# A fused attention, MLP and expert kernel on one core: a form of loads, two rules of its planner and its table of numbers are changed

## The chip, the cores and the metric

The kernel runs on one core of one Trainium2 chip. The core has a matrix engine (PE, with its weight loads PEld), a vector engine (DVE), a scalar engine (ACT), a general engine (POOL) and a queue for transfers (SP), which run side by side and wait for one another by semaphores. The metric is the device time of one execution in microseconds; the median of several runs counts.

## What is computed

Attention on (2, 8, 576, 64), a two-layer MLP with squared ReLU, and a sum over four experts weighted by normalised probabilities. In attention, the first four heads see the last 32 positions (local) and the other four the positions of the same residue modulo 32 (strided).

```python
scores = scale * np.matmul(q, k.transpose(0, 1, 3, 2))
mask_local = (rel >= 0) & (rel < stride)
mask_strided = (rel >= 0) & (pos[None, :] % stride == pos[:, None] % stride)
scores = np.where(masks[None, :, :, :], scores, -1000000000.0)
attn = softmax(scores)
x = np.matmul(attn, v)              # to (1152, 512)
h = np.maximum(x @ w_in, 0.0)       # (512, 2048)
x = h * h @ w_out                   # (2048, 512)
for e in range(4):                  # (512, 1024) and (1024, 512)
    out += p[:, e:e + 1] * (np.maximum(x @ w1[e], 0.0) @ w2[e])
```

## The kernel before

All work is written as tasks with costs and ranks, and a planner in the kernel (class Plan) plays them through when the program is built: each engine takes the ready task of lowest rank for which buffers are free, and the order so found is what each engine executes. The costs in it (SAME, CROSS, FROM_PE and so on are delays between engines in ns) are the author's numbers; they set the order and nothing else. The long table of numbers in the main function holds ranks, buffer counts and switches.

Attention is cut into twelve groups. A strided group covers eight heads times a few residues of one batch (54 or 36 rows of keys and queries in each unit, eight units); a local group covers 192 queries in six units. A group goes through these steps: k, q and v are loaded by SP (lines 459 to 469 for strided groups, 543 to 549 for local ones); PE forms scores (484, 564) into one PSUM bank, with the mask added either by a matmul of constants (478, 558; on_pe_) or by DVE (646, 650); DVE takes the maximum (657); the exponential is either whole (DVE subtracts, 666, ACT does one instruction, 667, DVE sums, 668) or unit by unit (ACT, 661, with the sum on the way); DVE makes the reciprocal (670), POOL or DVE normalises (671); PE transposes (489, 569, 571), ACT or DVE copies the result out (634); PE multiplies with v (501, 581, 586) into one or two banks; ACT and DVE write the result as a high part (682, 684) and a low part (688) into x. Five groups of the first batch are the start-up; five more (one local, three strided, one local) and two last local ones run between the products of the MLP. The start-up groups may use the ba and by banks, the later ones only the two ba banks.

The strided class has two forms. With four=True the v of a group is loaded in two transfers to 64 partitions each, and the value matmuls go to four places (two halves of the contraction by two halves of the output) and two banks. With four=False one transfer with zero padding fills 128 partitions, and the matmuls go to two places and one bank. The start-up uses False, the second batch True.

The MLP works on x in three blocks of 384 tokens (x0, x1, x2). A product is three matmuls (high times high, high times low, low times high; lines 883 to 885). Four products make one H in a bank bh (at first also by); ACT and DVE make the squared ReLU and its two halves h (948 to 961); h enters the second layer's sums in by (y products). Weights come as 512 KB loads into three buffers raw (828) and are split by ACT, DVE and POOL (834, 840, 845, 853, 855, 859). Later stages multiply blocks with fewer products by Strassen-like sums (lines from 1049 on, and the groups of the experts, whose results DVE adds in lines 1376 and 1543). While PE has nothing to do in the start-up the planner puts filler matmuls in (line 1572); their number is fixed when the program is built.

The rule that picks a bank when several rings can serve takes the first ring that has one. set_up (lines 420 to 427) makes the identity and the local masks from the constants cb on DVE; score tasks come after it in the plan.

Of the kernel before, what the change touches and what calls it, by code (L numbers as in the profile page):

```python
# [16 lines left out]
P = 128  # L17
# [56 lines left out]
class Plan:  # L74
# [8 lines left out]

    SAME, CROSS, FROM_PE, TO_PE, DMA = 40, 125, 205, 260, 2200
    FIRST_DMA = 700
# [6 lines left out]
    def __init__(self):  # L92
        self.tasks, self.rings = [], {}
        self.filler = None
        self.tense = set()
        self.shared = 0
# [15 lines left out]
    def run(self):  # L112
# [32 lines left out]
        while done < len(self.tasks):  # L145
# [4 lines left out]
            while events and events[0][0] == now:  # L150
# [4 lines left out]
                elif what == "idle":  # L155
                    idle[x] = True
                elif what == "end":
                    t = x
                    done += 1
                    for env, key in t.free:  # L160
                        ring, tile_ = env["_", key]
                        self.rings[ring].append(tile_)
                    for ring, tiles in t.adds:
                        self.rings[ring] += tiles
                    for y in then.get(t, ()):
                        waits[y] -= 1
                        if y.behind is t or t.ran == "pe" and "pe" in y.engines:
                            lag = 0
                        elif t.ran == "dma":
                            lag = self.DMA  # L170
                        elif t.ran in y.engines:
                            lag = self.SAME
                        else:
                            lag = self.FROM_PE if t.ran == "pe" else self.TO_PE if "pe" in y.engines else self.CROSS
                        ready_at[y] = max(ready_at.get(y, 0), now + lag)
                        if not waits[y]:
                            push(ready_at[y], "ready", (y, None))
            for e in ready:
                while idle[e] and ready[e]:
# [14 lines left out]
                    for env, key, rings in got.take:  # L194
                        r = next(r for r in rings if self.rings[r])
                        tile_ = self.rings[r].pop(0)
# [30 lines left out]
def tile_attention_mlp_experts(ctx: ExitStack, tc: tile.TileContext, a, out):  # L227
# [24 lines left out]
    HOLD = 4828  # L252
    AHEAD = 13299
    END2 = 34373
    END3 = -13679
    CONV = -36244
    R_LOW, R_HI = 5016, 616
    CONV1 = -36491
    CONV2 = 32503
    FETCH = 62728  # L260
    WITH2 = -2960
    PE_SLICE = 1914
    SQ = (0, 20, 0)
    R_MASK = 5624
    ON_PE = (1, 0, 0, 0, 0, 0, 0)
    FILL = 0
    R_MAX = 46387
    R_EXP = -28553
    R_NORM = 34851
    R_T = -64464  # L270
    R_V = -44215
    R_X = -42089
    R_LO = -58785
    R_OUT = -599
    FIRST = (-10664, -21928, 10634, -16154, -76519)
    WHOLE = (1, 1, 0, 0, 1, 1, 1, 1, 1, 1, 1, 0)
    S_T, S_V, S_X = -14699, 658, 1170
    L_T, L_V, L_X = 4928, -8176, -46841
    LKQ = (-9530, -55365, -19117, -7603, -3595)
    LV = (5544, -85907, 1533, 13101, 30113)  # L280
    LW = {('wi', 0, 1): -25050, ('wi', 0, 0): -59935, ('wi', 1, 1): -15643, ('wo', 0, 0): -58033, ('wo', 0, 1): -37919, ('wi', 1, 0): 812}
    EARLY = {('wi', 0, 1): -55765, ('wi', 0, 0): -53381, ('wi', 1, 1): 36780, ('wo', 0, 0): -20896, ('wo', 0, 1): -14224, ('wi', 1, 0): 12953}
    GROUP = 4
    AHEAD_H = 3
    EARLY_H = ((25994, -28049, -26801, 16069), (24535, -56810, 107537, 9733), (-57149, -14711, -28287, 25063), (-38851, -19584, 18159, -9722))
    NRAW = 3
# [6 lines left out]
    NV = 5  # L293
    LEAD = -27857
    L_CB = -31388
    L_ID = 18024
    WI1 = 11088
    NPT = 2
    NW = 10
    NS = 2  # L300
    NTMP = 3
    S_LEAD = -12738
    S_LEAD1 = -12772
    T_LEAD1 = 45954
    U = 2 * GROUPS
# [36 lines left out]
    def mm_r(n):  # L342
        return 229 if n == 512 else int(n / 2.4) + 13

# [64 lines left out]

    t_pe = plan.add({"dma": 500}, load_pe, rank=due(2 * half))  # L410
    t_pe = plan.add({"dve": 700}, weigh, after=[t_pe], rank=due(2 * half) + 8000)

# [191 lines left out]
    def attend(g, rank, rings, lead, early=None, whole=False, on_pe_=1):  # L604
# [33 lines left out]
        masked = on_pe_  # L638
        t = plan.add({"pe": g.cost_s + (mm_r(n) if masked else 0)}, lambda e: g.scores(env, masked), after=[t_cb, t_ci, t_go, *loads[:2], *(transposed[-3:-2] if len(rings) == 1 else [])], rank=rank, take=[(env, "S", rings)], free=[(env, "q"), (env, "k")], tiled=True)
        if not masked:  # L640
# [56 lines left out]
    for k, g in enumerate(startup):  # L697
        attend(g, FIRST[k], ["bank_a", "bank_y"], 0, k, WHOLE[k])
    second = [Local(0, 2)] + [Strided(1, j) for j in range(3)] + [Local(1, 0)]
    for k, g in enumerate(second):  # L700
# [5 lines left out]
    def open_late(e):  # L706
# [7 lines left out]
        for k in range(KD // 2):  # L714
            late["h", k] = late["T", 2][:, :, k]

    t_late = plan.add({"none": 1}, open_late, after=attention_done, rank=0, adds=[("parts", [("parts", 0)])])

# [557 lines left out]
    def open_last(e):  # L1276
        early.close()
        rp = ctx.enter_context(tc.tile_pool(name="last", bufs=1, side="right"))
        for k in range(3):
            late["w2", k] = rp.tile([P, 2, DM], F32R, name=f"o{k}")  # L1280

    t_last = plan.add({"none": 1}, open_last, after=t_sums, rank=0, adds=[("w2", [("w2", k) for k in range(3)]), ("tmp", [("tmp", 0)])])
# [379 lines left out]
```

## Time and profile before

| | us |
|---|---|
| median of 3 runs | 621.35 (620.80 to 621.83) |
| profiled execution | 621.1 |
| its span | 619.3 |
| PE busy | 609.3 (98%) |
| DVE busy | 458.7 (74%) |
| ACT busy | 301.5 (49%) |
| POOL busy | 122.7 (20%) |

The span is the time from the first to the last instruction that the profile shows. Busy time of PE counts overlapping matmuls once. In a time line a row has its start, its length, the engine, the source line, the operation and its tiles, and in square brackets the idle time before it and what ended it; "issue" stands there when the profile shows nothing that it waited for. The TensorE clock granted was at full speed from 4.6 us on.

### The profile page before, as it was taken

The page shows a single profiled execution, that of the slowest core. Times are in us where ns is not written, and L with a number is a line of the kernel's source. Part 1 is how long each engine was busy: PE and PEld are TensorE (multiplying, and loading weights), DVE is VectorE, ACT ScalarE, POOL GpSimd, SP SyncE. Part 2 cuts the span into 40 slices and gives each one's busy share as a digit, 9 for nine tenths or more (in the row PEclk, how much of TensorE's full clock was granted, in tenths as well). Part 3 has the DMA queues.
Part 4 walks back from the last instruction along what each step waited for, and adds up shares of the span by engine and source line. Part 5 has one row for each costly group of instructions (what it writes and reads, how often), then busy time and mean ns, then how long its engine had stood idle before and what let it go on. Part 6 is the DMA issues. An engine that isn't in the chain of part 4 may idle for free.

```text
span 619.3 us, 10613 instructions
## 1 busy us (share of the span) xinstructions
PE 609.3 (98%) x4026; PEld 556.5 (90%) x4026; DVE 458.7 (74%) x893; ACT 301.5 (49%) x688; POOL 122.7 (20%) x148
## 2 busy tenths in 40 slices
PE   8999999999999999999999999999999999999997
PEld 4788999999999999998898989898898989898996
DVE  5988897385787973978577785959877776978654
ACT  4675776555454643675244534344343534334330
POOL 2243330000010101033041221312141321313000
PEclk9999999999999999999999999999999999999999
DMA  8885314032222100020110202020210202030012
GB/s 309 276 248 214 125 49 137 1 131 73 69 68 69 36 1 15 3 85 19 39 54 15 81 18 87 17 86 17 64 31 17 79 17 86 19 85 1 0 52 102
DMA packets 35811, 44.80 MB, mean 72 GB/s; under 512 B 4016, under 2 KB 25392, under 8 KB 35760
## 3 DMA queue, kind: packets, MB, share of 16 engines
q1 hardware_dynamic: 35760, 44.13, 22.3%
q8 instruction: 31, 0.51, 0.3%
q14 instruction: 20, 0.16, 0.1%
HBM read 41.76 MB, written 2.36 MB: 71 GB/s over the span
## 4 chain that ended last, share of the span: by engine, by line
PE 88%; DVE 6%; DMA 3%; issue 1%; ACT 1%; SPq 1%; DVEq 0%
PE bh L883 11%; PE bh L885 10%; PE bh L884 10%; PE by L1424 10%; PE by L1425 10%; PE by L1423 10%; PE by L883 4%; PE by L885 4%; PE by L884 4%; PE ba L885 3%; PE ba L883 3%; PE ba L884 3%; DVE acc L1376 1%; DMA raw<-in_wo_dram 1%; DMA pe<-in_pe_dram 1%
## 5 line engine op out<-in xcount | busy, mean ns | idle before, releaser
L1376 DVE SCALAR_TENSOR_TENSOR acc<-by,pe,acc 128x512 f32<-128x512 f32 (+1 forms) x109 | 79.3, 741 | 20.9 <-PE by L1425 19.8
L883 PE MATMUL bh<-x,w 128*128 128x384 f32 x234 | 79.5, 340 | 1.7 <-DVE h L961 1.0
L885 PE MATMUL bh<-x,w 128*128 128x384 f32 x234 | 78.3, 335 | 0.0
L884 PE MATMUL bh<-x,w 128*128 128x384 f32 x234 | 78.3, 335 | 0.0
L1332 ACT ACTIVATE w<-sf 128x256 fp32r<-128x256 f32 x110 | 41.6, 408 | 58.7 <-POOL sf L1321 58.7
L1321 POOL TENSOR_TENSOR sf<-raw,raw 128x256 f32<-128x256 f32 x40 | 32.6, 823 | 189.0 <-DMA raw<-in_w_dram 116.5
L1424 PE MATMUL by<-o,h 128*128 128x512 f32 (+1 forms) x134 | 52.6, 392 | 0.0
L1425 PE MATMUL by<-o,h 128*128 128x512 f32 (+1 forms) x134 | 52.5, 392 | 0.0
L1423 PE MATMUL by<-o,h 128*128 128x512 f32 (+1 forms) x134 | 52.4, 391 | 0.0
L883 PE MATMUL by<-h,w 128*128 128x384 f32 x152 | 51.5, 339 | 0.0
L885 PE MATMUL by<-h,w 128*128 128x384 f32 x152 | 50.8, 334 | 0.0
L884 PE MATMUL by<-h,w 128*128 128x384 f32 x152 | 50.8, 334 | 0.0
L859 POOL TENSOR_TENSOR w<-val,w 128x512 fp32r<-128x512 f32 x18 | 23.8, 1325 | 118.2 <-ACT w L853 103.3
L883 PEld LDWEIGHTS bh<-x,w 128*128 128x128 f32 x234 | 43.9, 188 | 3.2 <-DVE h L961 1.3
L884 PEld LDWEIGHTS bh<-x,w 128*128 128x128 f32 x234 | 43.9, 188 | 0.5
L885 PEld LDWEIGHTS bh<-x,w 128*128 128x128 f32 x234 | 43.9, 188 | 0.0
L1356 DVE TENSOR_TENSOR o<-raw,o 128x512 fp32r<-128x512 f32 x30 | 21.4, 716 | 21.8 <-ACT o L1353 21.7
L884 PE MATMUL bh<-w,w 128*128 128x384 f32 x110 | 36.8, 334 | 0.0
L885 PE MATMUL bh<-w,w 128*128 128x384 f32 x110 | 36.8, 334 | 0.0
L883 PE MATMUL bh<-w,w 128*128 128x384 f32 x110 | 36.7, 334 | 0.0
L1353 ACT ACTIVATE o<-raw 128x512 fp32r<-128x512 f32 x30 | 18.7, 631 | 36.8 <-PE by L1425 36.3
L1543 DVE TENSOR_TENSOR r<-r,bh 128x384 f32<-128x384 f32 x50 | 27.6, 552 | 11.6 <-ACT r L1538 8.6
(311 smaller groups left out, 1602.9 us busy)
## 6 DMA issues: line engine op xcount, KB each, us to landing
raw<-in_wi_dram SPq DMA_DIRECT2D x16, 512.0 KB, 3.3
raw<-in_wo_dram SPq DMA_DIRECT2D x16, 512.0 KB, 4.1
raw<-in_w_dram SPq DMA_DIRECT2D x64, 128.0 KB, 2.7
raw<-in_w_dram SPq DMA_DIRECT2D x32, 256.0 KB, 2.8
out_dram<-acc SPq DMA_DIRECT2D x8, 256.0 KB, 2.0
v<-in_vl_dram SPq DMA_DIRECT2D x6, 256.0 KB, 6.1
k<-in_kl_dram SPq DMA_DIRECT2D x6, 224.0 KB, 5.3
q<-in_ql_dram SPq DMA_DIRECT2D x6, 192.0 KB, 5.5
```

Of the source, the lines that this page charges most:

```text
L859: eng[e].tensor_tensor(out=w[:, 1, cs], in0=value(), in1=f32(w[:, 0, cs]), op=ALU.subtract)
L883: nc.tensor.matmul(dst, lhsT=wh, rhs=xh, start=start, stop=False, skip_group_check=again)
L884: nc.tensor.matmul(dst, lhsT=wh, rhs=xl, start=False, stop=False, skip_group_check=again)
L885: nc.tensor.matmul(dst, lhsT=wl, rhs=xh, start=False, stop=stop, skip_group_check=again)
L1321: nc.gpsimd.tensor_tensor(out=value(dst), in0=value(x), in1=value(y), op=ALU.subtract if n in MINUS else ALU.add)
L1332: nc.scalar.activation(out=op_slot(env["op"])[:, 0].rearrange("p k f -> p (k f)"), in_=value(src), func=AF.Copy, scale=float(sign))
L1356: nc.vector.tensor_tensor(out=late[env["w2"]][:, 1], in0=f32(raws[f]["raw"][:, DM:]), in1=f32(late[env["w2"]][:, 0]), op=ALU.subtract)
L1376: nc.vector.scalar_tensor_tensor(out=acc, in0=o, scalar=pcol, in1=acc, op0=ALU.mult, op1=ALU.add)
L1423: nc.tensor.matmul(o, lhsT=h[:, 0, ts], rhs=w[:, 0], start=new, stop=False)
L1424: nc.tensor.matmul(o, lhsT=h[:, 0, ts], rhs=w[:, 1], start=False, stop=False)
L1425: nc.tensor.matmul(o, lhsT=h[:, 1, ts], rhs=w[:, 0], start=False, stop=stop)
L1543: nc.vector.tensor_tensor(out=at_(), in0=at_(), in1=bank["bank"][:, :TB], op=ALU.add if sign > 0 else ALU.subtract)
```

## The change

Six things are changed together.

- The three strided groups of the second batch use the form four=False: one load of v to all 128 partitions, one bank of results.
- Strided scores no longer come after the mask set-up in the plan, only local ones.
- The planner's bank rule: where a task may take bh or ba, it takes the one whose first bank has been free longest.
- Planner's delays between engines are a little different, and a step on DVE after one on DVE counts 118 and not 40 ns.
- The load of the expert weights pe and their normalisation come after all attention groups.
- The table of numbers is new: ranks, how long ahead loads are placed, which exponentials are whole (WHOLE), which squares ACT may do (SQ), where masks are added (ON_PE: the last local group's goes to PE), how many first H may use by banks (AHEAD_H). A dead tile named gap follows the last weight buffers.

```diff
-    SAME, CROSS, FROM_PE, TO_PE, DMA = 40, 125, 205, 260, 2200
+    SAME, CROSS, FROM_PE, TO_PE, DMA = 40, 118, 208, 270, 2200
+    AGAIN = 118
...
+                        self.since[id(tile_)] = now
...
-                            lag = self.SAME
+                            lag = self.AGAIN if t.ran == "dve" else self.SAME
...
-                        r = next(r for r in rings if self.rings[r])
+                        able = [r for r in rings if self.rings[r]]
+                        r = min(able, key=lambda r: self.since.get(id(self.rings[r][0]), 0)) if set(rings) == {"bank_h", "bank_a"} else able[0]
...
-    SQ = (0, 20, 0)
-    ON_PE = (1, 0, 0, 0, 0, 0, 0)
+    SQ = (2, 52, 1)
+    ON_PE = (1, 0, 0, 0, 0, 0, 1)
...
-    WHOLE = (1, 1, 0, 0, 1, 1, 1, 1, 1, 1, 1, 0)
+    WHOLE = (0, 1, 1, 0, 1, 0, 0, 1, 0, 1, 0, 1)
...
-    AHEAD_H = 3
+    AHEAD_H = 4
...
-    t_pe = plan.add({"dma": 500}, load_pe, rank=due(2 * half))
-    t_pe = plan.add({"dve": 700}, weigh, after=[t_pe], rank=due(2 * half) + 8000)
...
-        t = plan.add({"pe": ...}, lambda e: g.scores(env, masked), after=[t_cb, t_ci, t_go, ...
+        t = plan.add({"pe": ...}, lambda e: g.scores(env, masked), after=[t_cb, t_ci if g.kk == (0, 1) else None, t_go, ...
...
-    second = [Local(0, 2)] + [Strided(1, j) for j in range(3)] + [Local(1, 0)]
+    second = [Local(0, 2)] + [Strided(1, j, False) for j in range(3)] + [Local(1, 0)]
...
+    t_pe = plan.add({"dma": 2500}, load_pe, after=[x for x in attention_done], rank=due(2 * half))
+    t_pe = plan.add({"dve": 850}, weigh, after=[t_pe], rank=due(2 * half) + 8000)
...
+        rp.tile([P, 48], F32, name="gap")
```

Lines of the changed kernel are one to four higher than those of the kernel before (883 is 886, 501 is 502, 840 is 843, 845 is 848, 657 is 658).

DVE at the very start, before: set-up, two steps of the first weight (mid, val, raw), then the maxima st of scores in ba.

```order
L426 COPY first_73<-local_72 128x64
L427 MEMSET first_73 128x32
L840 TENSOR_SCALAR mid0_95<-mid0_95 128x512
L845 SCALAR_TENSOR_TENSOR val0_97<-raw0_92,mid0_95 128x512
L657 TENSOR_REDUCE st0_134<-ba0_107 128x8
L657 TENSOR_REDUCE st1_135<-ba1_108 128x8
L666 TENSOR_TENSOR p0_126<-ba0_107,st0_134 128x8x54
```

DVE at the same place, after:

```order
L427 COPY first_73<-local_72 128x64
L428 MEMSET first_73 128x32
L658 TENSOR_REDUCE st0_134<-ba0_107 128x8
L843 TENSOR_SCALAR mid0_95<-mid0_95 128x512
L667 TENSOR_TENSOR p0_126<-ba0_107,st0_134 128x8x54
L848 SCALAR_TENSOR_TENSOR val0_97<-raw0_92,mid0_95 128x512
L658 TENSOR_REDUCE st1_135<-ba1_108 128x8
```

The first maximum moved ahead of the two weight steps, and these stand between the steps of the groups.

PE around the first product of the MLP, before: the second local group's transposes (pl1) and values (pt0, v4) stand ahead of it.

```order
L586 MATMUL ba0_107<-pt0_132,v3_124 64x32 x8
L569 MATMUL by1_110<-ident_70,pl1_130 128x128 x2
L571 MATMUL by1_110<-ident_70,pl1_130 128x128 x2
L501 MATMUL by2_111<-pt1_133,v2_123 64x54 x16
L558 LDWEIGHTS cb_71
L558 MATMUL ba0_107<-local_72,cb_71 128x384
L564 MATMUL ba0_107<-k1_118,q1_114 32x64 x24
...
L586 MATMUL ba1_108<-pt0_132,v4_125 64x32 x8
L883 MATMUL bh0_105<-x0_77,w0_82 128x384
L884 MATMUL bh0_105<-x0_77,w0_82 128x384
```

PE around the first product, after:

```order
L587 MATMUL ba1_108<-pt1_133,v3_124 64x32 x8
L886 MATMUL bh0_105<-x0_77,w0_82 128x384
L887 MATMUL bh0_105<-x0_77,w0_82 128x384
L888 MATMUL bh0_105<-x0_77,w0_82 128x384
L886 MATMUL bh0_105<-x0_77,w0_82 128x384
L887 MATMUL bh0_105<-x0_77,w0_82 128x384
L888 MATMUL bh0_105<-x0_77,w0_82 128x384
L570 MATMUL by0_109<-ident_70,pl1_130 128x128 x2
L572 MATMUL by0_109<-ident_70,pl1_130 128x128 x2
L886 MATMUL bh1_106<-x0_77,w0_82 128x384
L887 MATMUL bh1_106<-x0_77,w0_82 128x384
L888 MATMUL bh1_106<-x0_77,w0_82 128x384
```

Two products now stand ahead of the second local group's transposes, and its values (pt0, v4) follow later still.

ACT ahead of the fifth H's relu, after (its rows before the change hold whole exponentials there):

```order
L662 ACTIVATE pl1_130,st0_134<-pl1_130,st0_134 128x64 x6
L635 ACTIVATE pt1_133<-ba0_107 128x512
L683 ACTIVATE x1_78<-ba1_108 128x2x6x8
L683 ACTIVATE x2_79<-ba1_108 128x24x8
L837 ACTIVATE mid1_96<-raw0_92 128x512
L951 ACTIVATE r0_103<-bh0_105 128x384
```

The unit-by-unit exponential of a local group (six activations) stands there ahead of the relu in ACT's fixed order.

## Rows read from the trace of the kernel before

**Rows 1.** the page's part 1: busy us, share of the span, instructions

```profile
...
PE 609.3 (98%) x4026; PEld 556.5 (90%) x4026; DVE 458.7 (74%) x893; ACT 301.5 (49%) x688; POOL 122.7 (20%) x148
...
```

**Rows 2.** who waited for whom on PE: us in total, times, longest

```profile
...
PE bh L883 <- DVE h L961: 1.0, 1, 1.0
...
PE bh L883 <- DVE r L1543: 0.7, 1, 0.7
...
```

**Rows 3.** time line of PE, 0 to 30 us: start, length, engine, line, operation

```profile
...
6.26 1.01 PE L484 MATMUL ba<-k,q 64*54 64x54 f32 x32
...
8.39 0.75 PE L484 MATMUL ba<-k,q 64*36 64x36 f32 x32 [0.89 <-DMA q<-in_qs_dram]
...
9.30 0.35 PE L478 MATMUL by<-cb 128*128 128x432 bf16 x1
...
15.45 0.30 PE L564 MATMUL by<-k,q 64*32 64x64 f32 x4 [0.78 <-issue]
...
16.62 2.54 PE L1572 MATMUL by<-idle 128*128 128x512 bf16 x11
19.08 1.14 PE L501 MATMUL ba<-pt,v 54*64 54x54 f32 x32
20.15 0.44 PE L569 MATMUL ba<-ident,pl 128*128 128x128 f32 x2
...
20.74 1.12 PE L501 MATMUL by<-pt,v 36*64 36x36 f32 x32
...
22.38 0.67 PE L581 MATMUL ba<-pt,v 64*64 64x32 f32 x32
...
23.57 0.44 PE L569 MATMUL by<-ident,pl 128*128 128x128 f32 x2
...
27.26 0.19 PE L581 MATMUL ba<-pt,v 64*64 64x32 f32 x1 [0.41 <-issue]
...
28.10 0.45 PE L883 MATMUL bh<-x,w 128*128 128x384 f32 x1
...
```

**Rows 4.** time line of DVE, 0 to 40 us

```profile
...
8.20 0.43 DVE L840 TENSOR_SCALAR mid<-mid 128x512 uint32<-128x512 uint32 x1 [1.08 <-ACT mid L834]
...
9.28 0.96 DVE L657 TENSOR_REDUCE st<-ba 128x8 f32<-128x432 f32 x2
...
26.04 0.45 DVE L688 TENSOR_TENSOR x<-by,x 128x288 fp32r<-128x288 f32 x1
...
```

**Rows 5.** time line of PE, 30 to 62 us

```profile
...
36.49 0.67 PE L581 MATMUL ba<-pt,v 64*64 64x32 f32 x32 [0.26 <-ACT pt L634]
...
42.92 0.69 PE L501 MATMUL ba<-pt,v 54*64 54x54 f32 x32
43.54 0.44 PE L883 MATMUL by<-h,w 128*128 128x384 f32 x1
...
44.17 0.33 PE L883 MATMUL by<-h,w 128*128 128x384 f32 x1
...
45.73 0.33 PE L883 MATMUL by<-h,w 128*128 128x384 f32 x1
...
54.34 0.69 PE L501 MATMUL ba<-pt,v 54*64 54x54 f32 x32 [0.57 <-ACT pt L634]
...
57.58 0.63 PE L489 MATMUL ba<-ident,p 128*128 128x128 f32 x4 [0.79 <-DVE x L688]
...
```

**Rows 6.** time line of ACT, 0 to 40 us

```profile
...
10.79 0.57 ACT L667 ACTIVATE p<-p 128x432 f32<-128x432 f32 x1 [1.49 <-DVE p L666]
11.26 0.27 ACT L661 ACTIVATE p<-ba,st 128x36 f32<-128x36 f32 x1
...
13.39 0.71 ACT L834 ACTIVATE mid<-raw 128x512 f32<-128x512 f32 x1
...
```

**Rows 7.** time line of SP's queue, 0 to 40 us

```profile
...
9.76 0.43 SPq L465 DMA_DIRECT2D v<-in_vs_dram  x1
...
29.08 2.50 SPq L469 DMA_DIRECT2D v<-in_vs_dram  x2
...
```

More of the change, by code (lines that the diff above doesn't have):

```diff
@@ L92, in __init__ @@
     def __init__(self):
-        self.tasks, self.rings = [], {}
+        self.tasks, self.rings, self.since = [], {}, {}
         self.filler = None
@@ L252, in tile_attention_mlp_experts @@
     HOLD = 4828
[L253 to L256, printed above, removed]
+    AHEAD = 2809
+    END2 = 32276
+    END3 = 22743
+    CONV = -12455
     R_LOW, R_HI = 5016, 616
[L258 to L261, printed above, removed]
+    CONV1 = -2094
+    CONV2 = -21191
+    FETCH = 2293
+    WITH2 = -804
     PE_SLICE = 1914
-    SQ = (0, 20, 0)
-    R_MASK = 5624
-    ON_PE = (1, 0, 0, 0, 0, 0, 0)
+    SQ = (2, 52, 1)
+    R_MASK = -90019
+    ON_PE = (1, 0, 0, 0, 0, 0, 1)
     FILL = 0
[L267 to L275, printed above, removed]
-    WHOLE = (1, 1, 0, 0, 1, 1, 1, 1, 1, 1, 1, 0)
+    R_MAX = 60717
+    R_EXP = -6260
+    R_NORM = -43877
+    R_T = -66773
+    R_V = -46019
+    R_X = -4784
+    R_LO = 19599
+    R_OUT = 1893
+    FIRST = (-51908, 5690, -68076, -11008, -71051)
+    WHOLE = (0, 1, 1, 0, 1, 0, 0, 1, 0, 1, 0, 1)
     S_T, S_V, S_X = -14699, 658, 1170
     L_T, L_V, L_X = 4928, -8176, -46841
[L279 to L282, printed above, removed]
+    LKQ = (-9582, -57000, -28496, -4543, -9486)
+    LV = (35741, -82185, 10475, 62786, 39756)
+    LW = {('wi', 0, 1): -46128, ('wi', 0, 0): -67495, ('wi', 1, 1): -80529, ('wo', 0, 0): -18922, ('wo', 0, 1): -75283, ('wi', 1, 0): -69308}
+    EARLY = {('wi', 0, 1): -81490, ('wi', 0, 0): -57267, ('wi', 1, 1): 22521, ('wo', 0, 0): -55570, ('wo', 0, 1): 29308, ('wi', 1, 0): -91630}
     GROUP = 4
-    AHEAD_H = 3
-    EARLY_H = ((25994, -28049, -26801, 16069), (24535, -56810, 107537, 9733), (-57149, -14711, -28287, 25063), (-38851, -19584, 18159, -9722))
+    AHEAD_H = 4
+    EARLY_H = ((-44017, -29595, -3498, -45849), (107894, 71042, -29046, -81860), (39084, -19275, -56971, -80754), (4063, -19712, -54508, 10171))
     NRAW = 3
@@ L293, in tile_attention_mlp_experts @@
     NV = 5
[L294 to L297, printed above, removed]
+    LEAD = -77782
+    L_CB = -84794
+    L_ID = -25921
+    WI1 = 1466
     NPT = 2
@@ L301, in tile_attention_mlp_experts @@
     NTMP = 3
-    S_LEAD = -12738
-    S_LEAD1 = -12772
-    T_LEAD1 = 45954
+    S_LEAD = 30323
+    S_LEAD1 = -2800
+    T_LEAD1 = 353
     U = 2 * GROUPS
@@ L342, in mm_r @@
     def mm_r(n):
-        return 229 if n == 512 else int(n / 2.4) + 13
+        return 228 if n == 512 else int(n / 2.4) + 13
     def act(n):
@@ L638, in attend @@
         masked = on_pe_
-        t = plan.add({"pe": g.cost_s + (mm_r(n) if masked else 0)}, lambda e: g.scores(env, masked), after=[t_cb, t_ci, t_go, *loads[:2], *(transposed[-3:-2] if len(rings) == 1 else [])], rank=rank, take=[(env, "S", rings)], free=[(env, "q"), (env, "k")], tiled=True)
+        t = plan.add({"pe": g.cost_s + (mm_r(n) if masked else 0)}, lambda e: g.scores(env, masked), after=[t_cb, t_ci if g.kk == (0, 1) else None, t_go, *loads[:2], *(transposed[-3:-2] if len(rings) == 1 else [])], rank=rank, take=[(env, "S", rings)], free=[(env, "q"), (env, "k")], tiled=True)
         if not masked:
```

## The prediction

> **What bounds the kernel now.** I read the shares of busy time first, then who waited for whom on PE, then the time line of the first 60 us. In [rows 1] PE is busy for 609.3 of 619.3 us, so what other engines save counts only where PE stands still or does work that need not be there. PE's two largest waits on DVE late in the program are 1.0 us for a low half h (line 961) and 0.7 us for r (line 1543) [rows 2]; in the stretch where MLP products and attention are mixed it waited 0.26, 0.57 and 0.79 us [rows 5]. The other lever is the time before the first product of the first MLP layer, the "first product" below (a product is three matmuls, on lines 883 to 885), at 28.10 us [rows 3]. From there PE's pace is fixed: nine matmuls took 45.73 - 44.17 = 1.56 us, 0.173 us each [rows 5].
>
> **How the sum is made.** The profiled execution took 621.1 us, its span was 619.3, so 1.8 us lie around the span. The median of the three runs shown is 621.35, 0.25 us above the profiled one. I work out differences against the profiled trace and put them on the median. 0.2% is 1.24 us, about what a measurement of this kernel can tell from no change: below 620.1 is faster, above 622.6 slower.
>
> **Start-up.** From the second strided group's scores (8.39 us, PE had waited for their q) to the first product PE's list is nearly the same work before and after, and its order shows what differs. Before there are 21 filler matmuls (line 1572) in it, after 20. Eleven fillers take from 16.62 to 19.08 us, 0.224 us each [rows 3], so one fewer is -0.2 us. Then two waits: PE stood 0.78 us inside the second local group's score matmuls and 0.41 us inside a group's value matmuls [rows 3], for nothing that the profile shows; both lie in runs of very short matmuls while DMA was full, so the instructions themselves may have come late, and then such a wait can follow the short matmuls to their new places. Of the 1.2 us I count 1.0 as gone. Last, the second local group's transposes and value matmuls now stand behind the first two products. That brings the first product forward by 20.74 - 20.15 = 0.59 and 23.57 - 22.38 = 1.19 us [rows 3], 1.8 us in all, and gives nothing by itself, as PE does them later. So the start-up is worth -1.2 us, and the first product should start at 28.1 - 1.2 - 1.8 = 25.1 us.
> Are its operands there by then? DVE wrote the last strided piece of x0 at 26.04 us for 0.45 us, and PE used it 1.6 us later [rows 3, 4]. The piece was DVE's 45th instruction from its first reduction of scores and is now the 44th, with two more weight steps inside that count (a shift and the step on line 845) and fewer steps of the local groups. The first reduction itself stood behind those two weight steps: the shift waited 1.08 us for ACT and began at 8.20, the reduction at 9.28 [rows 4], of scores that PE had finished at 7.27 (6.26 + 1.01 [rows 3]). Now it can begin near 7.3. So x0 can come up to 2 us earlier, at 24.5 by the end of its 0.45 us, which just covers 25.1; if it comes only 1 us earlier, PE waits 0.4 us. Bounds for the start-up: -2.4 (the first scores 1 us earlier too, as the constants lead SP's queue) and +0.4 (x0 as late as now, and the two waits replaced by one).
>
> **Value loads and value matmuls.** The three strided groups of the second batch now load v in one zero-padded whole-partition transfer of 256 KB, not in two halves of 128 KB: the same bytes. On SP's queue two halves took up to 2.50 us to issue, a whole one 0.43 [rows 7]. The weight loads stand behind them on SP, so weights come earlier; but no weight is among PE's large waits, so I count 0 on the path. If weights were late, it would be up to 2 us for a group.
> The matmuls cost PE more, all of it on the path: 32 of the new form, which the start-up has used all along, took 20.15 - 19.08 = 1.07 us, 32 of the old form 43.54 - 42.92 = 0.62 us [rows 3, 5]. Three groups: 3 x 0.45 = +1.35 us. The Trainium skill (TensorEngine Tiling (Array Packing), section Available Configurations) says that a 64x64 configuration holds four independent tiles; the form that goes used all four, the new one two, and by that rule its cost would double, to 3 x 0.62 = +1.9 us, and the sum be 0.5 us higher. The rows measured 1.07 for the new form, so they decide.
> In return the results fill one bank and not two. Second-batch groups have only the two ba banks for scores, transposes and results, so the old form needed both at once. The waits of 0.57 us (values, for the copy pt) and 0.79 us (the next transposes, for DVE's last reader x) are of these groups [rows 5], and x has half as many readers now. With the 0.26 us that is 1.6 us of early waits.
>
> **Which engine does what.** Of the seven later groups four do their exponentials unit by unit by the table WHOLE (before, one). Each takes a subtraction and a sum off DVE, about 0.5 us apiece as the two reductions at 9.28 (0.96 us together [rows 4]), and gives ACT 13.39 - 11.26 = 2.13 us for eight units in place of 0.57 [rows 6]; six units at the same price are 1.6. DVE's squares (line 955) fall from 20 to 14. DVE and ACT only count through PE's waits, so this is no term of its own: it is why I let 1.5 of the 1.6 us of early waits go. Bounds -1.6 and 0.
> The last group's mask goes from DVE to PE: one matmul more, at most the 0.35 us of such a matmul [rows 3], pipelined a little less: +0.3.
>
> **Oldest bank first.** A product that may take bh or ba now takes the bank that has been free longest. The wait of 0.7 us on r is a product whose bank bh was still being read by DVE's line 1543, so this is where it should help; the 1.0 us on h is a step that has bh alone, with DVE late. I count 1.2 of the 1.7 us as gone, bounds -1.7 and 0. That strided scores don't wait for the mask set-up moves nothing by itself: PE multiplied the bf16 constants at 9.30 [rows 3] and needs only their load. The expert weights pe move behind attention, off SP's queue and DVE in the busy stretch: 0 on the path, since nothing needs them before the experts' outputs.
>
> **Sum.** -1.2 (start-up) + 1.35 (value matmuls) + 0.3 (mask) - 1.5 (early waits) - 1.2 (late waits) = -2.25 us: 621.35 - 2.25 = **619.1 us**. All terms at their low bounds: -2.4 + 1.35 + 0.3 - 1.6 - 1.7 = -4.05, or 617.3, and 616.7 with the half microsecond by which the runs differ. All at their high bounds: +0.4 + 1.35 + 0.35 = +2.1.
>
> **Rivals.**
> A, the front gains nothing: x0 comes no earlier than now, and waits of the old size stand elsewhere. It gives back the 1.2 and half of the early waits: 619.1 + 1.2 + 0.75 = 621.05. For it: DVE has little to spare there, and x0's cover is only 0.6 us. Against it: the first reduction clearly comes free. It decides if x0's piece is written after 26 us.
> B, ACT becomes the bound, slower: three more groups run unit by unit, 2 x (2.13 - 0.57) + (1.6 - 0.57) = 4.2 us more on ACT, in a fixed order, in the stretch after the start-up. A finished H waits for ACT's relu; PE can go on with the other bh bank for one H alone, 12 x 0.173 = 2.08 us, and an exponential of eight units is longer than that. It decides where a relu stands close behind one with no y products on PE meanwhile. All of it exposed: 619.1 + 4.2 = 623.3. For it: in ACT's new order the fifth H's relu stands five instructions behind a six-unit exponential. Against: the other groups' pieces and the y products keep PE busy there, and ACT is busy for 49% of the span [rows 1].
> C, the change does not do what it says: one result bank and the oldest bank free nothing, and the waits of 1.6 and 1.7 us stay: 619.1 + 1.5 + 1.2 = 621.8.
>
> **Chances.** The forecast with its own range, 616.7 to 620.1: 0.66. A 0.12 and C 0.08, both no change. B 0.14. So faster 0.66, same 0.20, slower 0.14. The range, 616.7 to 621.9, takes in the forecast, A and C with their spread, and leaves B out.
>
> **What would show it.** Right: the first product near 25.1 us with no wait over 0.3 us in front of it; 32 value matmuls of the second batch in 1.07 us; no waits of 0.5 us or more on pt and x before 80 us; no 0.7 us on r. Wrong: the first product after 26.5 us (A); a wait of over 1 us on ACT's r or on an h whose relu came late (B); 3 us of PE's waits still there behind the first product (C).

## The result: 614.8 us, and a profile in which PE is quicker as well as less idle

The changed kernel takes **614.82 us**, the median of four runs (613.95 to 615.65), against 621.31 us for the kernel before beside it: a ratio of 0.9895, 95% interval 0.9878 to 0.9913, so 6.5 us less (5.4 to 7.6). On another chip it took 614.44 us against 620.76, ratio 0.9903 (0.9887 to 0.9919). The forecast was 619.1 us, range 616.7 to 621.9: the sign was right, the gain nearly three times the forecast one, and the time lies below the range.

Part 1 of the page of the changed kernel (busy us, share of the span, instructions) and its span, beside [rows 1]:

```profile
span 613.9 us, 10601 instructions
...
PE 606.5 (99%) x4025; PEld 558.6 (91%) x4025; DVE 446.8 (73%) x872; ACT 307.9 (50%) x729; POOL 127.5 (21%) x153
...
```

PE is still the bound, busy for 606.5 of 613.9 us. Its instructions are one fewer than before, yet its busy time fell by 2.8 us: waits ending sooner don't do that. The waits themselves, by who waited for whom on PE (us in total, times, longest), beside [rows 2, 5]:

```profile
...
PE ba L485 <- DMA q<-in_qs_dram: 2.4, 1, 2.4
PE by L1576 <- DVE idle L1580: 1.0, 1, 1.0
PE ba L570 <- DVE pl L667: 0.5, 1, 0.5
PE by L1427 <- DVE acc L1380: 0.2, 1, 0.2
PE by L565 <- issue: 0.2, 1, 0.2
```

The 1.0 us on h and the 0.7 us on r are gone, as are the early ones on pt and x; 0.5 us on pl (at 59 us) and 0.2 us on acc (at 422 us) are new. The wait for q is the start-up's; this profile shows it at its worst (2.4 us). A second profile of the changed kernel, from the run called after_again below, has 1.2 and 0.9 us there and a span of 612.3 us. I use it for the account, since it is nearer to the median run.

**The account.** I add up, from either trace, the distances from the start of each PE instruction to the start of the next. They end at the start of the last one, 615.63 us before and 608.89 us now. Standing still is what a distance has beyond its usual length, a little more than the idle time that a view gives:

| PE's time, us | before | changed (after_again) | difference | forecast |
|---|---|---|---|---|
| up to the first product | 28.10 | 25.70 | -2.40, of which 1.78 only moved behind it: -0.62 | -1.2 |
| attention's small matmuls behind it, with the change-overs | 15.81 | 18.82 | +3.01, of which 1.78 moved there: +1.23 | +1.65 |
| standing still, 28 to 80 us | 2.02 | 0.54 | -1.48 | -1.5 |
| standing still, later | 2.46 | 0.39 | -2.07 | -1.2 |
| 2,100 matmuls of 384 columns (883 to 885) | 366.34 | 366.14 | -0.20 | 0 |
| 873 matmuls, most of 512 columns (1423 to 1425) | 200.91 | 197.30 | **-3.61** | 0 |

The first four rows, all that the prediction put into its sum, make -2.94 us, against a forecast of -2.25. The last row is the rest, and the prediction has no term for it. So the question for the experiments was why the same 873 matmuls became quicker.

The trace of before already held the answer's first half. The groups of instructions by line and form (x count | busy us, mean ns of one | idle) in two stretches, 262 to 269 us and 302 to 307 us, of the kernel before:

```profile
...
L1423 PE MATMUL by<-w,h 128*128 128x512 f32 x8 | 3.1, 389 | 0.0
...
```

```profile
...
L1425 PE MATMUL by<-o,h 128*128 128x512 f32 x6 | 2.4, 396 | 0.0
...
```

The same instruction took 389 ns where its moving operand is the tile w and 396 ns where it is o. (Two groups of three in the first view stand at 395 and 396 with w too: they are the first matmuls of a run, see the table below.) The pace shows it as well; the time line of the kernel before, line 1423 alone, which is every third matmul, and of its rows the first and the fourth:

```profile
...
321.45 0.40 PE L1423 MATMUL by<-o,t 128*128 128x512 f32 x1
...
323.55 0.39 PE L1423 MATMUL by<-o,h 128*128 128x512 f32 x1
```

Nine matmuls in 323.55 - 321.45 = 2.10 us, 233 ns each. The 54 that read w, ahead of 283 us, follow each other at 228 ns on average.

### The profile page after: what moved, and what is told of

Its sections match the earlier page's. It is cut to its first block, busy times and chain, and to the rows that moved or that the text cites. A ratio compares the mean times of both kernels' runs of the same rounds, so it can differ in the third digit from the quotient of the medians.

```text
span 613.9 us, 10601 instructions
## 1 busy us (share of the span) xinstructions
PE 606.5 (99%) x4025; PEld 558.6 (91%) x4025; DVE 446.8 (73%) x872; ACT 307.9 (50%) x729; POOL 127.5 (21%) x153
## 4 chain that ended last, share of the span: by engine, by line
PE 96%; DVE 1%; DMA 1%; issue 0%; SPq 0%
PE by L1428 11%; PE by L1429 11%; PE by L1427 11%; PE bh L886 9%; PE bh L888 9%; PE bh L887 9%; PE ba L888 6%; PE ba L886 6%; PE ba L887 6%; PE by L886 5%; PE by L888 5%; PE by L887 5%; PE by L1576 1%; PE ba L485 1%; DMA q<-in_qs_dram 1%; PE ba L502 1%
## 5 line engine op out<-in xcount | busy, mean ns | idle before, releaser
L886 PE MATMUL bh<-x,w 128*128 128x384 f32 x194 | 65.8, 339 | 0.0
L888 PE MATMUL bh<-x,w 128*128 128x384 f32 x194 | 64.9, 335 | 0.0
L887 PE MATMUL bh<-x,w 128*128 128x384 f32 x194 | 64.9, 334 | 0.0
L1429 PE MATMUL by<-o,h 128*128 128x512 f32 (+1 forms) x131 | 50.8, 388 | 0.0
L1428 PE MATMUL by<-o,h 128*128 128x512 f32 (+1 forms) x131 | 50.8, 388 | 0.0
L1427 PE MATMUL by<-o,h 128*128 128x512 f32 (+1 forms) x131 | 50.5, 386 | 0.0
L1325 POOL TENSOR_TENSOR sf<-sf,raw 128x256 f32<-128x256 f32 x40 | 32.5, 821 | 22.2 <-DVE w L1344 21.9
L886 PEld LDWEIGHTS bh<-x,w 128*128 128x128 f32 x194 | 36.4, 188 | 0.4
L887 PEld LDWEIGHTS bh<-x,w 128*128 128x128 f32 x194 | 36.4, 188 | 0.2
L888 PEld LDWEIGHTS bh<-x,w 128*128 128x128 f32 x194 | 36.4, 188 | 0.0
L1342 DVE TENSOR_TENSOR w<-sf,w 128x256 fp32r<-128x256 f32 x80 | 31.8, 417 | 2.1 <-ACT w L1336 2.1
L951 ACT ACTIVATE r<-bh 128x384 f32<-128x384 f32 x30 | 14.7, 491 | 35.0 <-PE bh L888 34.9
L1449 ACT ACTIVATE h<-r 128x384 fp32r<-128x384 f32 x26 | 13.7, 526 | 36.7 <-DVE r L1547 36.5
```

The source lines that it names most:

```text
L886: nc.tensor.matmul(dst, lhsT=wh, rhs=xh, start=start, stop=False, skip_group_check=again)
L887: nc.tensor.matmul(dst, lhsT=wh, rhs=xl, start=False, stop=False, skip_group_check=again)
L888: nc.tensor.matmul(dst, lhsT=wl, rhs=xh, start=False, stop=stop, skip_group_check=again)
L1325: nc.gpsimd.tensor_tensor(out=value(dst), in0=value(x), in1=value(y), op=ALU.subtract if n in MINUS else ALU.add)
L1342: eng[e].tensor_tensor(out=l, in0=value(src), in1=f32(h), op=ALU.subtract)
L1427: nc.tensor.matmul(o, lhsT=h[:, 0, ts], rhs=w[:, 0], start=new, stop=False)
```

## The experiments

Theory **G** says: the unused tile `gap`, one line of the diff that the prediction passed over, moved the three tiles o by 192 bytes, and their address sets PE's pace. Rival **H**: an unused tile does nothing, and the pace came with the new order of work.

**gap_alone**, the kernel before with that line alone:

```
         for k in range(3):
             late["w2", k] = rp.tile([P, 2, DM], F32R, name=f"o{k}")
+        rp.tile([P, 48], F32, name="gap")
```

> The kernel before with one line of the change: the unused tile of 48 columns (192 bytes) behind the three tiles o of the last pool, which moves their addresses and nothing else; the order of the instructions is that of before. Theory G (the address of the moving operand sets PE's pace): before, the 54 products on lines 1423 to 1425 ahead of 283 us, which read other tiles, follow each other at 227 to 229 ns, the 819 behind, which read o, at 233 ns on average; with the tile these go at 228 too, 819 x 4.8 ns = 3.9 us less, so 617.4 us. Rival H (the tile does nothing, and the other pace comes from the new order of work): 233 ns as before, 621.3 us.

Measured: 618.15 us (616.85 to 618.65) against 621.01, ratio 0.9953 (0.9939 to 0.9966): -2.9 us. Its time line at the place shown for before:

```profile
...
320.73 0.39 PE L1425 MATMUL by<-o,t 128*128 128x512 f32 x1
...
322.77 0.39 PE L1425 MATMUL by<-o,h 128*128 128x512 f32 x1
...
```

Nine matmuls in 2.04 us, 227 ns each, with PE's order unchanged. H falls.

**no_gap**, the changed kernel without the line:

```
-        rp.tile([P, 48], F32, name="gap")
```

> The changed kernel without the unused tile; its order of instructions stays. Theory G: 233 ns in place of 228 from 283 us on, 614.8 + 3.9 = 618.7 us, and that is what the rest of the change is worth, about -2.6 us, near the -2.25 us of the prediction's sum. Rival H: 614.8 us.

Measured: 618.15 us (616.85 to 618.26), ratio to before 0.9950 (0.9937 to 0.9962). So all the rest of the change is worth -3.1 us (-3.9 to -2.4) and the one line about as much again (614.8 us, on another chip, in place of 618.15). By the traces the line's 512-column matmuls account for 3.7 us here and 3.75 in gap_alone. Part of it is lost again in the 384-column ones, which take 0.7 us more in total in each of the two kernels with the line; why, no run tells. In gap_alone the wait on r is gone too.

**offsets_a** and **offsets_b** give the three tiles addresses with different remainders:

```
         for k in range(3):
             late["w2", k] = rp.tile([P, 2, DM], F32R, name=f"o{k}")
-        rp.tile([P, 48], F32, name="gap")
+            rp.tile([P, (8, 8, 8)[k]], F32, name=f"gap{k}")
```

with (16, 8, 32) in offsets_b.

> The changed kernel, with the unused tile replaced by one of 32 bytes behind each of the three tiles o, so that their addresses leave 128, 160 and 192 when divided by 256 (before: 224 for all three; after: 32 for all three). Theory G says that the pace follows the tile that is read: up to three paces among the products that read o, between 227 and 236 ns; rival H, one pace of 227 to 229 ns for all three.

> As the one before, with the addresses of the three tiles o leaving 0, 64 and 96 when divided by 256. Theory G: the pace again differs from tile to tile, and one of the offsets may be quicker than 227 ns; rival H: 227 to 229 ns for all three.

Measured, one run each: 617.96 and 616.02 us. None of the six remainders is quick (table below): neither H's 227 to 229 ns nor the quicker offset that G allowed came. Of the 2 us between the two runs 1.0 lies ahead of the first product (26.28 and 25.24 us). **main0** then moves everything else, and **all0** everything:

```
     pe_s = const.tile([P, NT // P], F32, name="pe_s")
+    const.tile([P, 56], F32, name="pad")
...
-        rp.tile([P, 48], F32, name="gap")
+        rp.tile([P, 56], F32, name="gap")
```

main0 has the first of these two edits, all0 both. Theory G1: the remainder of the moving tile alone decides; G2: its distance from the other operands does.

> The changed kernel with an unused tile of 224 bytes in front of x, w, h and what follows them, so that all these addresses leave 0 in place of 32 when divided by 256; the three tiles o stay at 32. Theory G1 (the remainder of the moving tile alone decides, and 32 is a good one): the products that read o stay at 227 to 229 ns, the 54 products of the same shape that read w move to about 233 ns, and the 384-column products may leave their 173.5 ns; 614.8 us or, by 1 ns for 2,100 of these, 2 us to either side. Theory G2 (it is the distance between the moving tile and the tile of the weights, which are at 32 too in the changed kernel): the products that read o go to 233 ns, the 54 stay at 228, the 384-column ones at 173.5; 614.8 + 3.3 = 618.1 us.

> As main0, with the unused tile behind o 32 bytes longer, so that o leaves 0 too: all operands again have the same remainder, 0 in place of 32. Theory G1: o at 0 is at 233 ns, as the one tile at 0 in offsets_b was; 618.1 us. Theory G2: 227 to 229 ns, 614.8 us.

Measured: main0 618.18 us (617.30 to 619.17), all0 614.11 us (614.00 to 615.36), against 620.24 us; ratios 0.9969 (0.9958 to 0.9981) and 0.9907 (0.9893 to 0.9922). G2 had said 618.1 and 614.8. The time lines, line 1428 alone, which is every third matmul: main0's that read w, main0's that read o, and all0's that read o:

```profile
...
263.04 0.39 PE L1428 MATMUL by<-w,h 128*128 128x512 f32 x1
...
263.72 0.39 PE L1428 MATMUL by<-w,h 128*128 128x512 f32 x1
...
```

```profile
...
319.36 0.39 PE L1428 MATMUL by<-o,t 128*128 128x512 f32 x1
...
320.06 0.40 PE L1428 MATMUL by<-o,t 128*128 128x512 f32 x1
...
```

```profile
...
319.20 0.39 PE L1428 MATMUL by<-o,t 128*128 128x512 f32 x1
...
319.88 0.39 PE L1428 MATMUL by<-o,t 128*128 128x512 f32 x1
...
```

Three matmuls that read w take 0.68 us, three that read o 0.70 in main0 and 0.68 in all0. Averages of all that read one tile, in ns from start to start (stalls left out), by what remains of the addresses (as the built program has them) when they are divided by 256:

| kernel | the other operands | o0, o1, o2 | pace |
|---|---|---|---|
| before, no_gap | 32 | 224, 224, 224 | 233, 233, 233 |
| changed, gap_alone | 32 | 32, 32, 32 | 230, 227, 227 |
| offsets_a | 32 | 128, 160, 192 | 233, 232, 233 |
| offsets_b | 32 | 0, 64, 96 | 233, 232, 232 |
| main0 | 0 | 32, 32, 32 | 233, 233, 233 |
| all0 | 0 | 0, 0, 0 | 230, 227, 227 |
| the 54 that read w, all kernels | as w | - | 228 |

No remainder is good in itself. The pace settles at 227 ns where o has that of the other operands, and stays at 231 to 234 where it has not. G2 holds, G1 falls. Which of the others counts (the weights of this product, those of the next, the results of DVE and ACT) isn't told apart, since they were moved together. Nor is 256 shown to be the divisor: 160 against 32 in offsets_a, a distance of 128, is slow, which rules out 128 and its parts, but no run rules out a larger one.

The 230 of o0 is not the tile's own. The matmuls that read o come in runs of 27, but for the last ones, and in the changed kernel the first nine of a run take 231 ns each and the other eighteen 227, also in the runs that read the three tiles in turn. One of these in after_again, line 1427, again every third matmul:

```profile
...
321.67 0.39 PE L1427 MATMUL by<-o,h 128*128 128x512 f32 x1
...
323.75 0.39 PE L1427 MATMUL by<-o,h 128*128 128x512 f32 x1
...
325.79 0.39 PE L1427 MATMUL by<-o,h 128*128 128x512 f32 x1
...
```

Nine matmuls in 2.08 us, then nine in 2.04. The other runs start with o0 alone, so o0 has more of the slow ones. The runs that read w do the same in every kernel, which makes their 228; before and in main0 the runs that read o never come down to 227. Why a run starts at 231 is open.

**The late waits.** Theory O: the rule of the oldest bank takes the wait on r away. Rival T: such waits come and go with the order that the table gives. **before_oldest** is the kernel before with the rule, **after_any_bank** the changed one without:

```
-                        r = next(r for r in rings if self.rings[r])
+                        able = [r for r in rings if self.rings[r]]
+                        r = min(able, key=lambda r: self.since.get(id(self.rings[r][0]), 0)) if set(rings) == {"bank_h", "bank_a"} else able[0]
```

> The kernel before with one part of the change: a product that may take either bank takes the one that is free longest (the planner makes its order anew with it). Theory O (the rule takes the late wait on r away): the wait of PE for r at 437 us goes, the one for h at 139 us, a step with bh alone, stays: 621.0 - 0.9 = 620.1 us. Rival T (these waits come and go with the order that the table of numbers gives, not with the rule): a wait of 0.5 us or more on r or elsewhere behind 250 us is still there, 621.0 us or more.

> The changed kernel without the rule of the oldest bank (order made anew). Theory O: a wait of 0.7 to 0.9 us on r comes back, 614.8 + 0.9 = 615.7 us. Rival T: no such wait, 614.8 us.

Measured: before_oldest 619.38 us (618.30 to 622.70) against 620.24, ratio 0.9991 (0.9976 to 1.0005): no difference that the runs tell. after_any_bank 616.61 us (616.14 to 617.50), 0.9945 (0.9930 to 0.9960), on the chip where all0 took 614.11. From their waits, before_oldest first:

```profile
...
PE bh L885 <- DVE h L963: 1.0, 1, 1.0
PE ba L491 <- DVE x L690: 0.8, 1, 0.8
...
PE ba L503 <- ACT pt L636: 0.5, 1, 0.5
...
```

```profile
...
PE bh L885 <- DVE r L1546: 0.4, 1, 0.4
...
PE by L1426 <- DVE acc L1379: 0.2, 1, 0.2
```

In before_oldest no r is waited for any more, and the h of line 961, here 963, is, with 1.0 us, as O said. In after_any_bank r is back, at 434 us, with smaller stalls at 188, 204 and 537 us: PE stood 1.8 us behind the first product in place of 0.9. The kernel lost 2.5 us, more than O's 0.9; another 0.5 lies ahead of the first product (26.19 us, 25.68 in all0), the rest is open. But gap_alone lost its wait on r with no rule, by pace alone. So the rule does this, and isn't the only thing that does.

**The value form.** Theory V: the form costs 1.35 us and frees a bank that is worth 1.5 us of waits. Rival W: the waits belonged to the old order. **after_halves** puts the old loads and value matmuls back, **before_whole** puts the new ones into the kernel before (orders made anew; the start-up is unchanged in both):

```
-    second = [Local(0, 2)] + [Strided(1, j, False) for j in range(3)] + [Local(1, 0)]
+    second = [Local(0, 2)] + [Strided(1, j) for j in range(3)] + [Local(1, 0)]
```

and the reverse in before_whole.

> The changed kernel with the second batch's strided groups loading v in two halves again, with the four-tile form of the value matmuls that fills two banks (order made anew; the start-up up to the first product stays). Theory V (the terms of the prediction's sum: the form costs 1.35 us, and the bank that it leaves free takes 1.5 us of waits away): 3 x 32 matmuls at 0.62 in place of 1.07 us, waits of 0.5 us or more on pt and x back between 30 and 80 us, 614.8 - 1.35 + 1.5 = 615.0 us. Rival W (those waits came with the old order of work): no such waits, 613.5 us.

> The kernel before with the whole-partition value loads of the second batch alone (order made anew; the start-up up to the first product stays). Theory V: the waits of 0.57 us on pt and 0.79 us on x go and the value matmuls cost 1.35 us more, 621.0 + 1.35 - 1.5 = 620.9 us. Rival W: the waits stay, 621.0 + 1.35 = 622.4 us.

Measured: after_halves 616.91 us (616.31 to 618.66) against 614.44 of the same kernel without the edit, on one chip; before_whole 623.25 us (621.86 to 626.38) against 620.76, ratio 1.0050 (1.0029 to 1.0070). Both are 2.5 us worse, so neither theory's sum holds in either. In after_halves a wait on x came back, larger than the 0.79 us of [rows 5], with a new one on h, but none of 0.5 us on pt; the time line of PE, then of DVE and POOL:

```profile
...
49.18 0.87 PE L565 MATMUL ba<-k,q 64*32 64x64 f32 x48 [1.39 <-DVE x L689]
...
79.64 0.45 PE L886 MATMUL bh<-x,w 128*128 128x384 f32 x1 [1.03 <-DVE h L964]
...
```

```profile
...
47.50 1.42 DVE L843 TENSOR_SCALAR val<-mid 128x512 uint32<-128x512 uint32 x1
48.83 0.51 DVE L689 TENSOR_TENSOR x<-ba,x 128x144 fp32r<-128x144 f32 x2
```

```profile
...
46.11 2.52 POOL L862 TENSOR_TENSOR w<-val,w 128x512 fp32r<-128x512 f32 x2 [3.76 <-ACT w L856]
```

PE waits 1.39 us for the x that DVE writes at 48.83, behind a weight step that began at 47.50 and took 1.42 us while POOL was busy (two of its kind took 0.75 us together at 42.87). In all PE stood 3.6 us behind its first product, not 0.9. In before_whole the waits on pt and x went, as V said, but two on h came into their place; PE's time line, then stretches of 1 us (PE busy with its count, PEld, DVE, ACT, POOL, PE's granted clock, DMA):

```profile
...
46.85 0.44 PE L883 MATMUL by<-h,w 128*128 128x384 f32 x1 [0.45 <-ACT h L958]
48.21 0.62 PE L884 MATMUL by<-h,w 128*128 128x384 f32 x1 [0.92 <-DVE h L961]
...
```

```profile
...
48.00:49.00 1.00, 0.79 (x3) 0.64 (x4) 0.97 (x7) 0.00 (x0) 1.00 (x2) 0.66 0.91 176
49.00:50.00 1.00, 1.00 (x6) 1.00 (x5) 1.00 (x2) 0.00 (x0) 1.00 (x2) 0.50 0.91 360
...
51.00:52.00 1.00, 1.00 (x9) 0.60 (x10) 0.79 (x2) 0.71 (x2) 0.00 (x0) 0.64 0.24 98
...
```

0.45 and 0.92 us of standing still, and behind them the granted clock at 0.50, the 1.2 GHz level, for about 3 us. This is part of the 2.5 us: two of the kernel's seven runs had a mean granted clock of 1.00 and took 621.86 and 622.54 us, the other five 0.994 to 0.997 and 622.60 to 626.38. So the form and the order of DVE's work belong together: in the order that was made for it the form, with the mask, costs 1.2 us and the waits go; either half of the trade alone, each in an order made anew, costs 2.5, in before_whole partly by the clock.

**The start-up.** **after_again** repeats the changed kernel; **v_behind** differs from it in one transfer, and in nothing else of any engine's order:

```
+    LOADS = {(1, "v"): "", (1, "q"): "qv"}
...
-lambda e, w=what: g.load(env, w)
+lambda e, w=what: [g.load(env, x) for x in LOADS.get((early, w), w)]
```

> The changed kernel once more, as the measure for the three that share its chip: 614.8 us; the wait for the first q, 2.4 us in its one profile so far and 1.0 to 1.6 in those of its variants, nearer to 1.5, and the first product at 25.2 to 26.3 us.

> The changed kernel with the order of every engine as it is but for one transfer: the first strided group's v, which no score needs, is issued behind that group's k and q in place of ahead of them. Theory Q (PE's wait for the first q delays the whole start-up): q lands some 0.7 us sooner, as the transfer of v took 4.03 - 2.77 = 1.3 us of a busy queue at most and a q 0.4 to 0.6 at least; the first scores start 0.7 us sooner and so does the first product, 614.8 - 0.7 = 614.1 us. Rival F (what follows is paced by DVE and ACT or by the later loads): the first scores start sooner, the first product does not, 614.8 us.

Measured: 614.44 us (613.65 to 615.92) and 614.52 us (613.69 to 615.31). PE's time lines, after_again first:

```profile
...
6.54 1.01 PE L485 MATMUL ba<-k,q 64*54 64x54 f32 x32 [1.17 <-DMA q<-in_qs_dram]
...
9.58 0.75 PE L485 MATMUL ba<-k,q 64*36 64x36 f32 x32 [0.94 <-DMA q<-in_qs_dram]
...
25.70 0.44 PE L886 MATMUL bh<-x,w 128*128 128x384 f32 x1
...
```

```profile
...
5.73 1.03 PE L485 MATMUL ba<-k,q 64*54 64x54 f32 x32
...
9.19 0.75 PE L485 MATMUL ba<-k,q 64*36 64x36 f32 x32 [1.34 <-DMA q<-in_qs_dram]
...
25.81 0.44 PE L888 MATMUL bh<-x,w 128*128 128x384 f32 x1
...
```

The first scores start 0.8 us sooner and the first product does not, as F said. F's reason (DVE, ACT or the later loads) is not what the trace shows. At the second group's scores 0.39 us of the lead are left, and PE loses them inside the second local group's scores, for nothing that the profile shows, the place of the 0.78 us in [rows 3]; v_behind:

```profile
...
16.39 0.32 PE L565 MATMUL by<-k,q 64*32 64x64 f32 x8 [0.54 <-issue]
...
```

The DMA packets of the trace have a load of 16 KB, of the kind that they call instruction, which landed at 15.03 us, 1.36 us before PE went on. In the traces of all the kernels PE has sixteen waits marked issue, both of [rows 3] among them (loads landed at 14.12 and 26.01 us), and each ends 1.25 to 1.53 us behind the landing of such a load. That fits instructions of PE that came late; the packets don't tell for which engine a load is, and no run moved one. In these two profiles the wait for the first q costs nothing. None of these kernels is quicker than the changed one beyond what the runs tell.

## Why the prediction was right in sign and wrong in size

**What bounds the kernel.** "From there PE's pace is fixed" is the sentence that failed, and with it the part-by-part list, which has no entry for `gap`: the line's effect was put at nothing, without a reason, and it measured -3.6 us in the account and -2.9 us alone. The pace was read off one form, 0.173 us for 384 columns [rows 5]. The 512-column form had two paces in the same trace, 389 and 396 ns by its mean, and the diff had a line that moves the operand with the slow one. Had I asked why, the bounds would have reached 819 x (233 - 228) = 4 us below.

**Start-up**, forecast -1.2, measured -0.62, from one profile of each kernel (the first product comes at 28.24 to 28.59 us in the other kernels with the old start-up). The mechanism held in part: the first product starts at 25.70 us with no wait in front of it, in other profiles of the new order at 25.24 to 26.28, against the forecast 25.1; 20 fillers; the second local group's transposes and values behind the first two products. DVE's first reduction began at 7.58 us, x0's piece of 288 columns was written from 24.82 to 25.27 us:

```profile
...
7.58 0.61 DVE L658 TENSOR_REDUCE st<-ba 128x8 f32<-128x432 f32 x1 [3.14 <-PE ba L485]
...
24.82 0.45 DVE L689 TENSOR_TENSOR x<-by,x 128x288 fp32r<-128x288 f32 x1
...
```

against 9.28 and 26.04 in [rows 4]. So rival A, no earlier x0, is out in this profile, and in eight others of the new order, where that piece starts at 24.36 to 25.40 us. What was mis-sized is the start of the count. From the second strided group's scores to the first product it is 28.10 - 8.39 = 19.71 us before and 25.70 - 9.58 = 16.12 now, 1.81 less without the work that moved, more than the 1.2. But these scores begin 1.19 us later, as PE now waits for two q, 1.17 and 0.94 us, where it waited for one, 0.89; the sum had left their start where it was. Nor are the two waits counted as 1.0 us safely gone: such a wait ends when it does by the landing of an instruction load, as told above. This profile has none, v_behind, main0, offsets_a and after_any_bank have one of 0.54 to 0.85 us in the second local group's scores, as the prediction had said could happen. The profile of the page had a first product at 27.20 us, past A's mark of 26.5, and x0's piece at 26.32: PE had stood for 2.40 us from 4.94 on, and its clock fell, as the stretches of the changed kernel show:

```profile
...
6.00:7.00 1.00, 0.00 (x0) 0.00 (x0) 0.00 (x0) 0.00 (x0) 0.00 (x0) 1.00 0.91 299
7.00:8.00 1.00, 0.66 (x15) 0.69 (x17) 0.00 (x0) 0.00 (x0) 0.00 (x0) 0.68 0.98 346
8.00:9.00 1.00, 1.00 (x24) 0.90 (x20) 0.00 (x0) 0.50 (x1) 0.00 (x0) 0.50 1.06 358
...
10.00:11.00 1.00, 1.00 (x6) 0.20 (x5) 1.00 (x3) 0.91 (x2) 0.00 (x0) 0.62 1.02 392
11.00:12.00 1.00, 1.00 (x35) 0.81 (x35) 0.41 (x2) 0.17 (x1) 0.68 (x1) 1.00 1.02 355
...
```

**Value matmuls and mask**, forecast +1.65, measured +1.23. By lines, the value matmuls of the three groups went from 1.83 to 3.06 us, +1.23 against 1.35, and the mask's matmul took 0.27 against 0.3; the other small matmuls and the change-overs gave 0.27 back, which the prediction had not. The form's price was right: 64 of them in one row took 2.07 us, 1.03 per 32, where 1.07 was forecast:

```profile
...
45.26 2.07 PE L502 MATMUL ba<-pt,v 54*64 54x54 f32 x64
...
```

The doubling that the Trainium skill's rule gave, 1.24 us per 32, isn't what this row shows either: 1.03 over 0.62 [rows 5] is a factor of 1.7.

**Early waits**, -1.5 forecast, -1.48 measured, and the waits named are those that went. That the freed bank did it is only half shown: the bank's waits go in before_whole, but DVE's lateness takes their place unless the order suits.

**Late waits**, -1.2 forecast, -2.07 measured. The r wait went as said; the rule alone takes it away (before_oldest), and so did the new pace alone (gap_alone). The h wait of 1.0 us, which I had kept, went too. In before it follows a pair of DVE weight steps, which in the changed kernel takes 1.28 us; DVE and POOL of before:

```profile
...
137.32 2.38 DVE L788 TENSOR_TENSOR w<-sf,w 128x512 fp32r<-128x512 f32 x2
139.62 0.55 DVE L961 TENSOR_TENSOR h<-bh,h 128x384 fp32r<-128x384 f32 x1
```

```profile
...
137.73 1.42 POOL L859 TENSOR_TENSOR w<-val,w 128x512 fp32r<-128x512 f32 x1 [40.30 <-ACT w L853]
```

The pair took 2.38 us while POOL's step of 1.42 us ran, and h of line 961 stood behind it. The three kernels with the old order and no other value form (before, gap_alone, before_oldest) all have this wait, 0.97 to 0.99 us; those with the new order do not. That POOL stretched the pair, the whole trace of before bears out: of DVE's weight steps of 512 columns 72 ran with POOL idle, and none took over 0.69 us; 14 overlapped a POOL instruction, and 10 of them took longer than any of their kind with POOL idle. That the wait would go with the POOL step alone is argued from these rows; no run took that step away. **B** (ACT the bound) did not come: no wait on ACT's r or h in the changed kernel. **C** is out by the waits that are gone.

The four terms together were -2.25 forecast and -2.94 measured, -3.1 by no_gap's time. The missing term was as large as all of them together.

## What to carry to other kernels

When a trace has one form of matmul at two paces, ask which operand differs and look at its address: the matmuls that read three tiles ran 2% quicker here once the tiles' addresses left the same remainder by 256 as those of the other operands, and an unused tile of 192 bytes was worth as much as a re-planned order. Cost every line of a diff, also one that computes nothing. Where a wait has no releaser in the profile, see whether an instruction load landed just ahead of its end. A trade of one resource for another (a slower form for a free bank) is worth what the order around it makes of it: either half alone cost 2.5 us.

## What the runs showed of the hardware that I had not expected

PE's pace depends on where its operands lie in SBUF: 227 against 231 to 234 ns for 512 columns, with nothing else changed. The Trainium skill (SBUF — State Buffer, section SBUF: two separate sides) says that on the engines' side of SBUF only the port pair of VectorE and GpSimd causes contention and that PE never waits on anyone. Read as a pace of PE that nothing on that side changes, the measurement differs, and decides; whether PE meets another engine's accesses there or its own, no run tells. As to the pair, which the Trainium skill there calls an exclusive lock for a whole instruction, the traces fit it (2.38 us for a pair of 1.28, and 1.42 for a step of 0.4, beside POOL).

PE's clock fell after different pauses: after 2.40 us (the changed kernel's first profile: 0.68 in the stretch from 7 to 8 us, then 0.50) and after 0.45 and 0.92 us with one matmul between (before_whole); a single pause of 1.39 us in after_halves, ahead of 49.18 us, left it at 1.00:

```profile
...
48.00:50.00 2.00, 0.82 (x49) 0.73 (x49) 1.34 (x3) 2.00 (x13) 0.63 (x1) 1.00 0.81 190
...
```

One program doesn't always lose the clock either: of after_again's six runs three had a mean granted clock of 1.00 (613.65, 614.05 and 614.28 us) and three 0.997 (614.61, 615.83 and 615.92 us). So a wait's price is its length, or that and some microseconds at half pace behind it.
